# Running products in blocks of 8 joined in runs of four, and the second stage two blocks behind the first

## The chip, the cores and the metric

The kernel runs on one core of one Trainium2 chip. The metric is device time in microseconds of one execution; a stated time is the median of several runs. The engines named below are TensorE (PE; its weight loads are PEld), VectorE (DVE), ScalarE (ACT), GpSimd (POOL) and SyncE (SP), which here issues nearly all DMAs.

## The reference

There are 4 batches x 8 heads, 768 tokens and 48 channels per head. Each head keeps a complex 48x48 state that decays by a complex factor per channel and token:

```
scale = min(mag, 0.999) / (mag + 1e-6)        # mag = |a_re + i a_im|
a     = (a_re, a_im) * scale
for t in range(768):
    S    = a[t] * S  (complex, per channel)  + k[t] v[t]^T   (into the real part)
    y[t] = q[t] . Re(S)
x   = y as (3072 tokens, 384)
out = ((x @ w_a) * (x @ w_b)) @ w_out          # 384 -> 1536 -> 384
```

## The kernel before, in words

**Units.** The work is cut into 12 units u: 2 pairs of batches, each with 6 chunks of 128 tokens. A unit goes through two parts, attention and feed-forward. In attention the recurrence is replaced by matmuls: with P the running product of the factors `a` inside a chunk, the queries are multiplied by P and the keys divided by it, so that scores inside the chunk are q' . k', masked, and the state of the earlier chunks enters as one more matmul.

**`prep(u)`** makes P, on VectorE with help of ScalarE. A unit's factors are 128 partitions x 768 (six groups G of 128 tokens), in real and imaginary planes, plus a negated one (tile `z`). The first multiplication into `z` is L212, the negation L214. Then blocks of SUB = 16 tokens are multiplied up: for i from 1 to 15, one product of 192 elements (L228, into the tile `pr`) and one sum of 96 (L234) carry all 48 blocks of a unit (NB) one token further. In unit 0 each is done in two halves. Then the blocks are joined: 8 times (NSB), one after the other, a product of 24 elements (L255, `pb`) and a sum of 12 (L261, `b_t`) multiply the last value of a block into the carried state, for the six groups at once. L276 and L281 multiply every block's running products by the carried state. L284 to L308 make 1/P with ScalarE's help, L312 multiplies the keys, and L296 multiplies queries and keys by P into the tile `qk`. The last L296 ends the unit's prep.

**`scale(u)`** (L179 to L194) makes the factor `scale` of the next unit and is stepped along inside the loop over i.

**`stack(u)`** (L336) copies `qk` to the tile `stk`, in which each head has its own rows, by 10 DMAs on SP's queue (20 for units 0 and 1). **`attn(u)`** is a list of 12 or 18 pieces: scores (L369, masked by L372), transposes (L380, L384), outputs (L409, L413, with the rest in L418) and state (L426, L433).

**Feed-forward.** A pass over unit w has 12 blocks f of 128 hidden channels. The first stage (`gemm1`, L470) is 18 matmuls of 256 columns into the PSUM tile `ab`; ScalarE and VectorE then multiply the two halves and split the result in a high and a low part: `h_t` (L478, L479), `hh` (L480), `hl` (L481). The second stage (`gemm2`, L488) is 6 matmuls of 384 columns that add block f into the output tiles `o`. LAG = 3 says that the second stage of a block is issued when the first stage of the third block after it has been issued; HB = 4 is the number of buffers of `hh` and of `hl`.

**Weights** come packed and are split into a high and a low part at the start (`split_weights`): three VectorE instructions per piece (L135, L137, L139 into `o_sb`, 36 pieces, three per block f), a copy on ScalarE (L143), two matmuls (L148, L149) and a copy (L150). Pieces of 6 blocks are written ahead of the first attention, the others during pass 0.

**Order.** The program is written as an interleaving: in pass w stand the 12 blocks of unit w, the pieces of attention of unit w + 1, and the prep of unit w + 2 or w + 3, which a generator hands out in portions; the number after each `yield` is the cost that the portion is counted with. From that the tile framework's scheduler makes one order per engine, with priorities (`high_priority`) for what follows a matmul. Ahead of the attention of unit 1 stand WARM = 8 matmuls (L659, two records each) that read unit 1's `qk` and whose result nobody reads.

Of the kernel before, what the change touches and what calls it, by code (L numbers as in the profile page):

```python
# [8 lines left out]
F32 = mybir.dt.float32  # L9
# [5 lines left out]
ALU = mybir.AluOpType  # L15
# [7 lines left out]
NU = NBP * NCH  # L23
NJ = 3
G = 2 * NJ
SUB = 16
NSB = C // SUB
W = G * C
NB = G * NSB
PAIRS = [[2, NB], [2 * NB, SUB // 2], [1, 2]]  # L30
LIFT = 56
LN2 = 0.6931471805599453
# [8 lines left out]
RUN = 2 * TOK + 2  # L41
NF = DF // 128
KS = 2 * D
LAG = 3
EARLY = 2
WARM = 8
HB = 4
O_BUFS = 3
CONV_ON_AB = 7
NCHK = NU * G + NU + 1  # L50
# [9 lines left out]
def view(ap, offset, dims):  # L60
    return bass.AP(tensor=ap.tensor, offset=ap.offset + offset, ap=[list(ap.ap[0])] + dims)


def at_(i):
    return i // 2 * 2 * NB + i % 2


@with_exitstack
def tile_kernel(ctx: ExitStack, tc: tile.TileContext, a_d, qk_d, v_d, w_d, qn_d, kn_d, vn_d, an_d, out_d):
    nc = tc.nc  # L70
    vec, act, pe, sync = nc.vector, nc.scalar, nc.tensor, nc.sync
# [6 lines left out]
    small = fast.enter_context(tc.tile_pool(name="small", bufs=2))  # L78
# [119 lines left out]
    def rescaled(c):  # L198
        return c % 2 == 1 and c + 1 < NCH

    def prep(u):
# [7 lines left out]
        zz = z[:]  # L209

        for k in (1, 0):
            vec.tensor_tensor(out=view(zz, (1 + k) * W, PAIRS), in0=a_t[:, k].rearrange("p (b i e) -> p b i e", e=2, i=SUB // 2),  # L212
                              in1=sc.rearrange("p (b i e) -> p b i e", e=2, i=SUB // 2), op=ALU.mult)
        act.activation(out=z[:, 0], in_=z[:, 2], func=AF.Copy, scale=-1.0)  # L214
        yield 1700
        sg = scale(u + 1, a_tiles[u + 1], a_t) if 0 < u < NU - 1 else iter(())


        zb = z.rearrange("p s (j b e) -> p s j b e", j=SUB // 2, e=2)

        def tok(s, i, o, n):
            return zb[:, s, i // 2, o:o + n, i % 2]

        parts = [(p * NB // 2, NB // 2) for p in range(2)] if u == 0 else [(0, NB)]
        for i in range(1, SUB):
            pr = small.tile([128, 2, 2, NB], F32, name="pr", bufs=1)
            for o, n in parts:
                vec.tensor_tensor(  # L228
                    out=pr[:, :, :, o:o + n],
                    in0=view(zz, W + at_(i) + 2 * o, [[W, 2], [-W, 2], [2, n]]),  # L230
                    in1=tok(slice(1, 3), i - 1, o, n).unsqueeze(1).broadcast_to([128, 2, 2, n]),
                    op=ALU.mult)
            for o, n in parts:
                vec.tensor_tensor(out=tok(slice(1, 3), i, o, n), in0=pr[:, :, 0, o:o + n],  # L234
                                  in1=pr[:, :, 1, o:o + n], op=ALU.add)
            yield 440 + (next(sg, 0) if i > 3 else 0)
        for _ in sg:
            pass
        vec.tensor_scalar(out=tok(0, SUB - 1, 0, NB), in0=tok(2, SUB - 1, 0, NB), scalar1=-1.0,
                          scalar2=None, op0=ALU.mult)  # L240


        if c == 0:
            b_t = small.tile([128, 3, G, NSB], F32, name="b_t")
            vec.memset(b_t[:, 1, :, 0], 1.0)
            vec.memset(b_t[:, 2, :, 0], 0.0)
        else:
            b_t = bnext.pop(u)
# [1 line left out]
        if c + 1 < NCH:  # L250
            bn = bnext[u + 1] = small.tile([128, 3, G, NSB], F32, name="b_t")
        b8 = bn[:, 1:3, :, 0] if bn is not None and not rescaled(c) else small.tile([128, 2, G], F32, name="b8")[:]
        for sb in range(NSB):
            pb = small.tile([128, 2, 2, G], F32, name="pb")
            vec.tensor_tensor(  # L255
                out=pb,
                in0=view(zz, W + at_(SUB - 1) + 2 * sb, [[W, 2], [-W, 2], [2 * NSB, G]]),
                in1=b_t[:, 1:3, :, sb].unsqueeze(1).broadcast_to([128, 2, 2, G]),
                op=ALU.mult)
            dst = b_t[:, 1:3, :, sb + 1] if sb + 1 < NSB else b8  # L260
            vec.tensor_tensor(out=dst, in0=pb[:, :, 0], in1=pb[:, :, 1], op=ALU.add)  # L261
        vec.tensor_scalar(out=b_t[:, 0], in0=b_t[:, 2], scalar1=-1.0, scalar2=None, op0=ALU.mult)
        n2 = small.tile([128, 2, G], F32, name="n2")
        vec.tensor_tensor(out=n2, in0=b8, in1=b8, op=ALU.mult)
# [4 lines left out]
            act.activation(out=rho, in_=rho, func=AF.Exp, scale=-0.5, bias=b_rsq)  # L269
        yield 1600  # L270

        bb = b_t[:]
        for k in range(2):
            pz = a_t
            for s in range(2):
                vec.tensor_tensor(  # L276
                    out=pz[:, s].rearrange("p (j b e) -> p j b e", j=SUB // 2, e=2), in0=zb[:, 1 + s],
                    in1=view(bb, (1 + k - s) * NB, [[0, SUB // 2], [1, NB], [0, 2]]), op=ALU.mult)
            yield 1900

            vec.tensor_tensor(out=z[:, k].rearrange("p (b i e) -> p b i e", e=2, i=SUB // 2),  # L281
                              in0=view(pz[:], 0, PAIRS), in1=view(pz[:], W, PAIRS), op=ALU.add)
            yield 870
        act.activation(out=a_t, in_=z[:, 0:2], func=AF.Square)  # L284
        if rescaled(c):
            vec.tensor_tensor(out=bn[:, 1:3, :, 0], in0=b8,
                              in1=rho[:].unsqueeze(1).broadcast_to([128, 2, G]), op=ALU.mult)
# [13 lines left out]
        if u < EARLY:  # L301
            for k in range(2):
# [6 lines left out]
                                 op0=ALU.subtract, op1=ALU.mult, reverse0=True)  # L309
# [154 lines left out]
    def gemm1(f, xh, xl, ps_ab=ps_ab, moe=moe):  # L464
# [9 lines left out]
        h_t = moe.tile([128, TOK], F32, name="h_t")  # L474
        hh = moe.tile([128, TOK], F32, name="hh", bufs=HB)
        hl = moe.tile([128, TOK], F32, name="hl", bufs=HB)
        with tc.high_priority(offset=MOE_FIRST):
# [129 lines left out]
    ws = split_weights()  # L607
    drain(scale(0, a_tiles[0], z_first))
    drain(prep(0))
    stack(0)  # L610
    load_qk(1)
# [19 lines left out]
    for w in range(NU):  # L631
# [18 lines left out]
        for f in range(NF):  # L650
# [13 lines left out]
            slot()  # L664
            if len(pend) > LAG:
                second()
# [81 lines left out]
```

## Time and profile before

| what | value |
|---|---|
| median of 3 runs | 704.42 us (704.12 to 704.51) |
| the profiled execution | 705.48 us |
| its span, first to last instruction | 703.8 us |
| TensorE busy in the span | 655.8 us, 93%, 5854 matmul records |
| weight loads busy | 608.9 us, 87% |
| VectorE busy | 565.7 us, 80%, 1413 instructions |
| ScalarE busy | 310.4 us, 44%, 618 instructions |
| granted TensorE clock, mean | 0.965 |

A busy share is a mean over the whole span; the kernel has a start, in which weights are split and units 0 and 1 are prepared, a long middle, and an end without prep. So the profile is read by stretches of time: the table of stretches gives the busy time of each engine in each. A line of the trace's order in time gives start, length, engine, line, operation, the tile written and those read, and in brackets the engine's idle time just before with what ended it. "x16" merges 16 neighbours. Matmuls overlap, so that their records are longer than the distance from one to the next.

### The profile page before, as it was taken

To read this page: it belongs to the slowest core of one execution; us is meant where nothing else is said; L and a number is where in the kernel's file an instruction comes from. 1 tells how busy PE (TensorE), PEld (TensorE's weight loads), DVE (VectorE), ACT (ScalarE), POOL (GpSimd) and SP (SyncE) were. 2 spreads that over 40 slices of the span, in tenths; PEclk is the share of its full clock that TensorE was granted. 3 is DMA by queue.
4 is the path that set the end of the run, shared out by engine and by line. 5 is a ranking of instruction groups with operands and counts; after the bars stand their busy time and mean duration, and the time that the engine had idled before them with its cause. 6 is when DMAs were issued, how large, how long until landed. Compare 5 with 4: busy or idle time off the path is not lost.

```text
span 703.8 us, 14498 instructions
## 1 busy us (share of the span) xinstructions
PE 655.8 (93%) x5854; PEld 608.9 (87%) x5854; DVE 565.7 (80%) x1413; ACT 310.4 (44%) x618; POOL 5.6 (1%) x11
## 2 busy tenths in 40 slices
PE   3657999699999999999999999999999999999996
PEld 1224889599899899999899999999999999999996
DVE  6998899898888898889889989899899997233221
ACT  6347665534625525436346355362463323231221
POOL 3000000000000000000000000000000000000000
PEclk9566999899999999999999999999999999999999
DMA  8963300421512413305216043051250320400000
GB/s 320 401 253 88 118 1 1 137 75 45 159 31 75 129 32 108 110 17 158 65 26 190 16 125 95 31 163 42 76 157 2 102 87 9 114 23 2 23 1 28
DMA packets 32090, 63.95 MB, mean 91 GB/s; under 512 B 3984, under 2 KB 10640, under 8 KB 32016
## 3 DMA queue, kind: packets, MB, share of 16 engines
q1 hardware_dynamic: 28560, 58.23, 26.6%
q10 hardware_dynamic: 3456, 4.72, 1.9%
q8 instruction: 48, 0.79, 0.5%
q14 instruction: 26, 0.21, 0.1%
HBM read 39.32 MB, written 4.72 MB: 63 GB/s over the span
## 4 chain that ended last, share of the span: by engine, by line
PE 46%; DVE 42%; ACT 5%; DMA 3%; issue 3%; SPq 1%; DVEq 0%; ACTq 0%
PE ab L470 19%; PE o L488 9%; PE xp L409 6%; DVE pr L228 5%; PE pm L369 5%; DVE a_t L276 4%; DVE qk L296 4%; PE pm L426 3%; DVE h_t L479 3%; DVE z L234 3%; DVE hl L481 3%; DMA stk<-qk 2%; DVE z L281 2%; PE pm L380 2%; DVE pb L255 2%
## 5 line engine op out<-in xcount | busy, mean ns | idle before, releaser
L470 PE MATMUL ab<-xh,w 128*128 128x256 f32 x1728 | 334.1, 283 | 0.0
L470 PEld LDWEIGHTS ab<-xh,w 128*128 128x128 f32 x1728 | 275.6, 189 | 1.9 <-issue 1.2
L470 PE MATMUL ab<-xl,w 128*128 128x256 f32 x864 | 243.0, 281 | 0.0
L470 PEld LDWEIGHTS ab<-xl,w 128*128 128x128 f32 x864 | 162.5, 188 | 0.7 <-issue 0.4
L488 PE MATMUL o<-w,hh 128*128 128x384 f32 x576 | 152.5, 344 | 0.0
L478 ACT COPY h_t<-ab 128x256 f32<-128x256 f32 x144 | 53.4, 371 | 175.4 <-PE ab L470 175.1
L479 DVE TENSOR_TENSOR h_t<-ab,h_t 128x256 f32<-128x256 f32 x144 | 60.5, 420 | 58.3 <-ACT h_t L478 57.7
L488 PEld LDWEIGHTS o<-w,hh 128*128 128x128 f32 x576 | 96.3, 188 | 3.2 <-issue 3.2
L488 PE MATMUL o<-w,hl 128*128 128x384 f32 x288 | 97.7, 339 | 0.0
L480 ACT CAST hh<-h_t 128x256 fp32r<-128x256 f32 x144 | 58.1, 404 | 78.4 <-DVE h_t L479 77.9
L481 DVE TENSOR_TENSOR hl<-h_t,hh 128x256 fp32r<-128x256 f32 x144 | 60.6, 421 | 16.8 <-ACT hh L480 16.5
L228 DVE TENSOR_TENSOR pr<-z 128x192 f32<-128x192 f32 (+1 forms) x195 | 65.2, 341 | 5.6 <-ACT z L214 1.3
L369 PE MATMUL pm<-stk 128*128 128x128 f32 x384 | 56.4, 284 | 3.4 <-DMA stk<-qk 3.4
L369 PEld LDWEIGHTS pm<-stk 128*128 128x128 f32 x384 | 50.2, 195 | 8.1 <-issue 7.6
L148 PE MATMUL ab<-o_sb,ident 128*128 128x384 f32 x42 | 30.1, 817 | 27.9 <-DVE o_sb L139 27.9
L488 PEld LDWEIGHTS o<-w,hl 128*128 128x128 f32 x288 | 54.1, 188 | 0.2
L234 DVE TENSOR_TENSOR z<-pr 128x96 f32<-128x96 f32 (+1 forms) x195 | 47.2, 249 | 3.7
L276 DVE TENSOR_TENSOR a_t<-z,b_t 128x768 f32<-128x768 f32 x48 | 45.5, 953 | 0.0
L409 PE MATMUL xp<-am,v_t 128*32 128x128 f32 x768 | 43.1, 277 | 0.5 <-DVE am L372 0.5
L148 PEld LDWEIGHTS ab<-o_sb,ident 128*128 128x128 f32 x42 | 10.6, 292 | 37.6 <-DVE o_sb L139 27.9
L296 DVE TENSOR_TENSOR qk<-qk,z 128x1536 f32<-128x1536 f32 (+1 forms) x28 | 42.6, 1523 | 0.1
L372 DVE TENSOR_TENSOR am<-pm,mask 128x512 f32<-128x512 f32 x48 | 32.9, 686 | 6.0 <-PE pm L369 5.7
(100 smaller groups left out, 753.9 us busy)
## 6 DMA issues: line engine op xcount, KB each, us to landing
w<-in_dram SPq DMA_DIRECT2D x36, 384.0 KB, 8.0
qk<-in_dram SPq DMA_DIRECT2D x12, 768.0 KB, 4.9
a_t<-in_dram SPq DMA_DIRECT2D x11, 768.0 KB, 4.4
stk<-qk SPq DMA_DIRECT2D x42, 192.0 KB, 3.3
v_t<-in_dram SPq DMA_DIRECT2D x24, 256.0 KB, 2.7
out_dram<-o_sb ACTq DMA_DIRECT2D x24, 192.0 KB, 2.0
stk<-qk SPq DMA_DIRECT2D x18, 192.8 KB, 3.3
stk<-qk SPq DMA_DIRECT2D x14, 128.0 KB, 3.0
```

Of the source, the lines that this page charges most:

```text
L228: vec.tensor_tensor(out=pr[:, :, :, o:o + n], in0=view(zz, W + at_(i) + 2 * o, [[W, 2], [-W, 2], [2, n]]), in1=tok(slice(1, 3), i - 1, o, ...
L234: vec.tensor_tensor(out=tok(slice(1, 3), i, o, n), in0=pr[:, :, 0, o:o + n], in1=pr[:, :, 1, o:o + n], op=ALU.add)
L276: vec.tensor_tensor(out=pz[:, s].rearrange("p (j b e) -> p j b e", j=SUB // 2, e=2), in0=zb[:, 1 + s], in1=view(bb, (1 + k - s) * NB, [[0, ...
L296: vec.tensor_tensor(out=qk4[:, :, k, x0:x1], in0=qk4[:, :, 1, x0:x1], in1=z[:, k].rearrange("p (j t) -> p j t", j=NJ).unsqueeze(2).broadca ...
L369: pe.matmul(out=sp[:, h4], lhsT=stk[:, h, ks], rhs=stk[:, h, qs], start=True, stop=True)
L409: pe.matmul(out=xp[qd * 32:(qd + 1) * 32, ti], lhsT=l, rhs=rr, start=st, stop=sp_, tile_position=(0, qd * 32), skip_group_check=True)
L470: pe.matmul(out=ab[:, m * TOK:(m + 1) * TOK], lhsT=r(w_ab(f, part, m * NJ + i)), rhs=r(xt[:, i, :]), start=n == 0, stop=n == 8)
L478: act.copy(out=h_t, in_=ab[:, 0:TOK])
L479: vec.tensor_tensor(out=h_t, in0=ab[:, TOK:2 * TOK], in1=h_t, op=ALU.mult)
L480: act.copy(out=r(hh), in_=h_t)
L481: vec.tensor_tensor(out=r(hl), in0=h_t, in1=hh, op=ALU.subtract)
L488: pe.matmul(out=os_[tt][:, 0:DM], lhsT=r(ht[:, ts]), rhs=r(w_t[f, 2][:, part, :]), start=(f == 0 and n == 0), stop=(f == NF - 1 and n == 2))
```

## The change

Three things change.

**Blocks of 8.** SUB goes from 16 to 8. The loop over i has 7 steps in place of 15, each over 96 blocks (NB) in place of 48: products of 384 elements and sums of 192. The number of blocks in a group of 128 tokens (NSB) goes from 8 to 16.

**The join in runs of four.** The 16 blocks of a group are four runs of RUNS = 4. First the running products inside every run are made for all 24 runs (NG) at once, in the new tile `c_t`: a copy, three times a product of 96 and a sum of 48, and a negation. Then the state is carried from run to run, four times a product of 24 and a sum of 12. At last the state inside the runs is filled in: two products and one sum of 144 elements. `joined` is the new helper that writes a product and a sum.

**The second stage.** LAG goes from 3 to 2 and HB from 4 to 3: the second stage of a block is issued after the first stage of the second block behind it, and `hh` and `hl` have three buffers each.

The count after a step's `yield` goes from 440 to 880, and `scale` is stepped along from the second step on.

```diff
-SUB = 16
+SUB = 8
+RUNS = 4
 NSB = C // SUB
 W = G * C
 NB = G * NSB
+NG = NB // RUNS
...
-LAG = 3
+LAG = 2
...
-HB = 4
+HB = 3
...
-            yield 440 + (next(sg, 0) if i > 3 else 0)
+            yield 880 + (next(sg, 0) if i > 1 else 0)
...
-        for sb in range(NSB):
-            pb = small.tile([128, 2, 2, G], F32, name="pb")
-            vec.tensor_tensor(
-                out=pb,
-                in0=view(zz, W + at_(SUB - 1) + 2 * sb, [[W, 2], [-W, 2], [2 * NSB, G]]),
-                in1=b_t[:, 1:3, :, sb].unsqueeze(1).broadcast_to([128, 2, 2, G]),
-                op=ALU.mult)
-            dst = b_t[:, 1:3, :, sb + 1] if sb + 1 < NSB else b8
-            vec.tensor_tensor(out=dst, in0=pb[:, :, 0], in1=pb[:, :, 1], op=ALU.add)
+        c_t = small.tile([128, 3, RUNS, NG], F32, name="c_t", bufs=1)
+        cc, bb = c_t[:], b_t[:]
+
+        def joined(out, x, y, n):
+            pb = small.tile([128, 2, 2, NG], F32, name="pb")
+            vec.tensor_tensor(out=pb[:, :, :, 0:n], in0=x,
+                              in1=y.unsqueeze(1).broadcast_to([128, 2, 2, n]), op=ALU.mult)
+            vec.tensor_tensor(out=out, in0=pb[:, :, 0, 0:n], in1=pb[:, :, 1, 0:n], op=ALU.add)
+
+        vec.tensor_copy(out=c_t[:, 1:3, 0], in_=view(zz, W + at_(SUB - 1), [[W, 2], [2 * RUNS, NG]]))
+        for k in range(1, RUNS):
+            joined(c_t[:, 1:3, k], view(zz, W + at_(SUB - 1) + 2 * k, [[W, 2], [-W, 2], [2 * RUNS, NG]]),
+                   c_t[:, 1:3, k - 1], NG)
+        vec.tensor_scalar(out=c_t[:, 0], in0=c_t[:, 2], scalar1=-1.0, scalar2=None, op0=ALU.mult)
+        n_run = NSB // RUNS
+        for k in range(n_run):
+            dst = b_t[:, 1:3, :, (k + 1) * RUNS] if k + 1 < n_run else b8
+            joined(dst, view(cc, NB + (RUNS - 1) * NG + k, [[NB, 2], [-NB, 2], [n_run, G]]), b_t[:, 1:3, :, k * RUNS], G)
+        pr = small.tile([128, 2, 2, RUNS - 1, NG], F32, name="pr", bufs=1)
+        for k in range(2):
+            vec.tensor_tensor(out=pr[:, k], in0=view(cc, (1 + k) * NB, [[-NB, 2], [NG, RUNS - 1], [1, NG]]),
+                              in1=view(bb, NB, [[NB, 2], [0, RUNS - 1], [RUNS, NG]]), op=ALU.mult)
+        vec.tensor_tensor(out=view(bb, NB + 1, [[NB, 2], [1, RUNS - 1], [RUNS, NG]]),
+                          in0=pr[:, :, 0], in1=pr[:, :, 1], op=ALU.add)
```

The scheduler makes a new order for every engine from the changed program. Lines behind the join lie 16 further down in the changed kernel: L296 becomes L312, L470 becomes L486, L488 becomes L504, L659 becomes L675; L228 and L234 become L230 and L236, and the weight splitting's L135, L137, L139 become L137, L139, L141. What the new order does on VectorE and TensorE around the end of unit 1's prep is shown in rows in the prediction, each row an instruction with its line, its operation, the tile it writes and those it reads.

More of the change, by code (lines that the diff above doesn't have):

```diff
@@ L270, in prep @@
         yield 1600
-        bb = b_t[:]
         for k in range(2):
```

## The prediction

> **What bounds the kernel now.** I read the page for the span, then the table of stretches, the order in time of TensorE and VectorE around the places where TensorE stops, and the matmuls of one feed-forward pass (12 blocks of 18 matmuls) per stretch. The table's columns: length, then busy time and instructions of PE, PEld, DVE, ACT and POOL, then TensorE's clock, DMA share and GB/s.
>
> ```profile
> span 703.8 us, 14498 instructions
> ...
> 0.00:61.00 61.00, 32.12 (x57) 14.54 (x57) 54.02 (x173) 32.07 (x62) 5.60 (x11) 0.72 0.79 293
> ...
> 80.00:126.00 46.00, 45.26 (x298) 40.60 (x297) 43.42 (x126) 28.76 (x60) 0.00 (x0) 1.00 0.08 25
> ...
> 154.00:330.00 176.00, 172.83 (x1633) 166.68 (x1632) 155.16 (x369) 80.42 (x155) 0.00 (x0) 1.00 0.28 83
> ```
>
> Up to 61 us VectorE is the full engine and TensorE waits. After 154 us TensorE is full. In between stands one long stop, in TensorE's order in time (start, length, what, idle time before it):
>
> ```profile
> 125.02 0.34 PE L488 MATMUL o<-w,hl 128*128 128x384 f32 x1
> 130.78 6.41 PE L659 MATMUL pm<-qk,ident 128*128 128x256 f32 x16 [5.42 <-DVE qk L296]
> ```
>
> TensorE has run out of blocks and waits 5.42 us for VectorE's last product of unit 1. So up to 130.7 us each microsecond off VectorE's queue counts; what TensorE still has to do behind the stop counts too. Then the passes, cut at their first matmul (216 matmul records, first length, then their busy time):
>
> ```profile
> 154.20:205.30 51.10, 28.57 (x216) 26.93 (x216) 1.00 0.28 81
> 205.30:257.65 52.35, 29.13 (x216) 27.11 (x216) 1.00 0.27 79
> 257.65:310.20 52.55, 28.68 (x216) 27.07 (x217) 1.00 0.28 83
> 310.20:358.05 47.85, 27.74 (x216) 26.84 (x217) 1.00 0.30 86
> ...
> 508.60:559.00 50.40, 27.80 (x216) 26.52 (x217) 1.00 0.27 75
> ...
> 610.10:656.05 45.95, 27.45 (x216) 26.76 (x217) 1.00 0.03 10
> ```
>
> A pass with 18 attention pieces beside it takes 50.40 where nothing is late; passes 1, 2 and 3 take 0.70, 1.95 and 2.15 more. Pass 4 has 12 pieces and takes 1.90 more than the other pass with 12, at 610 us. These 6.7 us are all that faster VectorE work can bring after 154 us, and the reason stands ahead of the scores:
>
> ```profile
> 180.75 0.46 PE L369 MATMUL pm<-stk 128*128 128x128 f32 x2 [1.25 <-DMA stk<-qk]
> ...
> 230.37 0.46 PE L369 MATMUL pm<-stk 128*128 128x128 f32 x2 [0.86 <-DMA stk<-qk]
> ...
> 280.42 0.46 PE L369 MATMUL pm<-stk 128*128 128x128 f32 x2 [1.05 <-DMA stk<-qk]
> ```
>
> The copy qk to stk starts when VectorE ends a unit's last product; there VectorE is late. From pass 5 on there is no such wait.
>
> **Running products.** VectorE's order in time, first unit 0 (two halves, weight work between), then unit 1 among other work, then unit 2 with nothing between:
>
> ```profile
> 19.87 0.43 DVE L228 TENSOR_TENSOR pr<-z 128x96 f32<-128x96 f32 x2 [0.30 <-ACT z L214]
> 20.22 0.33 DVE L234 TENSOR_TENSOR z<-pr 128x48 f32<-128x48 f32 x2
> 20.46 0.55 DVE L139 SCALAR_TENSOR_TENSOR o_sb<-w,o_sb 128x384 uint32<-128x384 uint32 x1
> ```
> ```profile
> 85.84 0.35 DVE L228 TENSOR_TENSOR pr<-z 128x192 f32<-128x192 f32 x1
> 86.11 0.35 DVE L135 TENSOR_SCALAR o_sb<-w 128x384 uint32<-128x384 uint32 x1
> 86.38 0.25 DVE L234 TENSOR_TENSOR z<-pr 128x96 f32<-128x96 f32 x1
> 86.54 0.55 DVE L137 SCALAR_TENSOR_TENSOR o_sb<-w,o_sb 128x384 uint32<-128x384 uint32 x1
> 87.01 0.35 DVE L228 TENSOR_TENSOR pr<-z 128x192 f32<-128x192 f32 x1
> ```
> ```profile
> 132.69 0.36 DVE L228 TENSOR_TENSOR pr<-z 128x192 f32<-128x192 f32 x1
> 133.09 0.26 DVE L234 TENSOR_TENSOR z<-pr 128x96 f32<-128x96 f32 x1
> 133.38 0.36 DVE L228 TENSOR_TENSOR pr<-z 128x192 f32<-128x192 f32 x1
> ```
>
> What an instruction costs is the step from its start to the next start: among other work 0.27 for 192 elements (85.84 to 86.11), 0.16 for 96, 0.47 for 384 (86.54 to 87.01), less than the durations; where the next one reads its result, 0.40 and 0.29.
>
> Unit 0: 15 steps of 0.35 + 0.24 = 0.59 make 8.9. After, 7 steps of twice 192 and twice 96 elements, 2 x (0.27 + 0.16) = 0.86, make 6.0: -2.9. Unit 1: 15 x (0.27 + 0.16) = 6.5 against 7 x (0.47 + 0.27) = 5.2: -1.3.
>
> The Trainium skill (VectorE: DVE Perf Modes, The DRAIN you can't avoid) says that the next op does not start until the pipe is empty, so that each instruction would cost its whole duration. Here 86.11 stands against it: the next instruction starts 0.27 after one that lasts 0.35. By the rule the saving would be larger; that is a rival below.
>
> **The join.** Before, 8 products of 24 elements and 8 sums of 12 per unit:
>
> ```profile
> 34.99 0.20 DVE L255 TENSOR_TENSOR pb<-z,b_t 128x24 f32<-128x24 f32 x1
> 35.10 0.55 DVE L139 SCALAR_TENSOR_TENSOR o_sb<-w,o_sb 128x384 uint32<-128x384 uint32 x1
> ...
> 35.57 0.17 DVE L261 TENSOR_TENSOR b_t<-pb 128x12 f32<-128x12 f32 x1
> 35.65 0.55 DVE L137 SCALAR_TENSOR_TENSOR o_sb<-w,o_sb 128x384 uint32<-128x384 uint32 x1
> ```
> ```profile
> 151.36 0.20 DVE L255 TENSOR_TENSOR pb<-z,b_t 128x24 f32<-128x24 f32 x1
> 151.59 0.18 DVE L261 TENSOR_TENSOR b_t<-pb 128x12 f32<-128x12 f32 x1
> ```
>
> Among other work a pair costs 0.11 + 0.08, 8 make 1.5. After: a copy and a negation (0.1 each), 3 products of 96 (0.16) and 3 sums of 48 (0.12, between 0.08 and 0.16), 4 of the old pairs (0.8), 3 instructions of 144 elements (0.22, between 0.16 and 0.27): 2.5, so +1.0 per unit, an estimate from these rows. Units 0 and 1 together save 2.9 + 1.3 - 2.0 = 2.2. That is the low bound of what the stop at 130.78 gains.
>
> **What the new order moves on VectorE.** Around unit 1's last product (qk<-qk,z), before:
>
> ```order
> L479 TENSOR_TENSOR h_t<-ab,h_t 128x256
> L290 TENSOR_TENSOR a_t<-a_t 128x768
> L481 TENSOR_TENSOR hl<-h_t,hh 128x256
> L306 TENSOR_TENSOR a_t<-a_t 128x768
> L308 SCALAR_TENSOR_TENSOR a_t<-a_t 128x768
> L312 TENSOR_TENSOR qk<-qk,a_t 128x3x256
> L296 TENSOR_TENSOR qk<-qk,z 128x3x256 x2
> L212 TENSOR_TENSOR z<-a_t,sc 128x48x8x2 x2
> ```
>
> and after, where o_sb<-w is weight splitting and L312 is the old L296:
>
> ```order
> L312 TENSOR_TENSOR qk<-qk,z 128x3x256
> L137 TENSOR_SCALAR o_sb<-w_194 128x384
> L312 TENSOR_TENSOR qk<-qk,z 128x3x256
> L495 TENSOR_TENSOR h_t<-ab,h_t 128x256
> L139 SCALAR_TENSOR_TENSOR o_sb<-w_194,o_sb 128x384
> L137 TENSOR_SCALAR o_sb<-w_196 128x384
> L497 TENSOR_TENSOR hl<-h_t,hh 128x256
> L141 SCALAR_TENSOR_TENSOR o_sb<-w_194,o_sb 128x384
> L139 SCALAR_TENSOR_TENSOR o_sb<-w_196,o_sb 128x384
> L137 TENSOR_SCALAR o_sb<-w_198 128x384
> L141 SCALAR_TENSOR_TENSOR o_sb<-w_196,o_sb 128x384
> L139 SCALAR_TENSOR_TENSOR o_sb<-w_198,o_sb 128x384
> ```
>
> Before, all weight splitting and 11 pairs h_t, hl stood ahead of that product; now 8 weight instructions (one more follows these rows) and one pair stand behind it. The 8 cost 2 x 0.27 + 6 x 0.47 = 3.4, the pair (256 elements, between 0.27 and 0.47) 0.7. Other weight instructions now stand between L290 and L306, where before VectorE waited:
>
> ```profile
> 125.79 0.96 DVE L306 TENSOR_TENSOR a_t<-a_t 128x768 f32<-128x768 f32 x1 [1.70 <-ACT a_t L292]
> ```
>
> I take 1.0 of these 1.70 as filled, bounds 0 and 1.70. The stop so ends 2.2 + 3.4 + 0.7 + 1.0 = 7.3 earlier, bounds 2.2 and 8.0. What went behind is not late again: TensorE first runs 6.41 us of L659, longer than these 4.1.
>
> **What the second stage's new place moves on TensorE.** Around the same stop, o<-w the second stage and pm<-qk the matmuls that wait. Before:
>
> ```order
> L488 MATMUL o_794<-w_960,hh 128x384 x2
> L488 MATMUL o_794<-w_960,hl 128x384
> L488 MATMUL o_795<-w_960,hh 128x384 x2
> L488 MATMUL o_795<-w_960,hl 128x384
> L488 MATMUL o_794<-w_1019,hh 128x384 x2
> L488 MATMUL o_794<-w_1019,hl 128x384
> L488 MATMUL o_795<-w_1019,hh 128x384 x2
> L488 MATMUL o_795<-w_1019,hl 128x384
> ```
>
> These are blocks 8 and 9, block 10 follows, then the stop. After:
>
> ```order
> L504 MATMUL o_741<-w_905,hh 128x384 x2
> L504 MATMUL o_741<-w_905,hl 128x384
> L504 MATMUL o_742<-w_905,hh 128x384 x2
> L504 MATMUL o_742<-w_905,hl 128x384
> L675 MATMUL pm<-qk,ident 128x256 x8
> L150 MATMUL pm<-o_sb,ident 128x384
> L151 MATMUL pm<-w_1100,nident 128x384
> ```
>
> Only block 8 is done ahead of the stop; blocks 9 and 10 come behind it, where TensorE is full. The chain of waits gives what a block costs there, first and second stage:
>
> ```profile
> 613.50 2.12 PE ab L470 x18
> 615.62 1.05 PE o L488 x6
> ```
>
> So 2 x 1.05 = 2.1 is given back, and the start gains 7.3 - 2.1 = 5.2.
>
> **Later units.** With nothing between, 15 x (0.40 + 0.29) = 10.4 becomes 7 steps of about 0.59 (a 384-element instruction, 0.55, plus the same 0.04) + 0.40, that is 6.9: -3.4. The join, 16 x 0.23 = 3.7, becomes about 4.8: +1.1. So a unit saves 2.3 there, and 1.3 - 1.0 = 0.3 among other work; I take 1.1, nearer the second, since VectorE is busy 155.16 of 176. VectorE enters unit 2 only 7.3 - 3.4 = 3.9 earlier, plus 1.1 makes 5.0, and TensorE 5.2: the wait of pass 1 stays. In passes 2, 3 and 4 the copies come 1.1 earlier each time, which they can use up (1.95, 2.15, 1.90): -3.3, bounds 0 and 6.7. Passes from 5 on gain nothing: TensorE hides VectorE's work. Fewer buffers for hh and hl cost nothing: block f writes where f-3 was read, and that second stage now stands ahead of block f's first.
>
> Sum: 703.8 - 5.2 - 3.3 = 695.3 of span. The profiled execution took 705.48, 1.7 outside its span; the median is 704.42, so I predict 704.42 - 8.5 = 695.9.
>
> **Rivals.** (1) The order's gain is lost (TensorE waits for the weight work put behind): the stop gains 2.2 and gives back 2.1, leaving 704.4 - 0.1 - 3.3 = 701.0. For it: block 11's weights now stand between the stop and the first scores. Against: the 6.41 us of cover.
>
> (2) Nothing: VectorE's time is hidden and the score waits are set by the copies: 704.4. Against: 5.42 us named after VectorE.
>
> (3) Slower: the second stage two blocks behind finds hl late, and TensorE waits in each block. From a first stage's end it now has 1.05 + 2.12 + 1.05 + 2.12 = 6.3 us. The slowest block in the late passes:
>
> ```profile
> 372.76 0.28 PE L470 MATMUL ab<-xh,w 128*128 128x256 f32 x1
> ```
> ```profile
> 377.99 0.42 DVE L481 TENSOR_TENSOR hl<-h_t,hh 128x256 fp32r<-128x256 f32 x1
> ```
>
> 373.04 to 378.41 is 5.4, so 0.9 is left. It decides from 6.3 on: at a mean of 6.5 the 96 blocks of passes 0 to 7 lose 0.2 each, 19 us, and the time is 715.1.
>
> (4) Whole durations count, with no overlap between starts:
>
> ```profile
> L228 DVE TENSOR_TENSOR pr<-z 128x192 f32<-128x192 f32 x165 | 58.9, 357 | 5.3 <-ACT z L214 1.0
> ...
> L234 DVE TENSOR_TENSOR z<-pr 128x96 f32<-128x96 f32 x165 | 42.3, 257 | 3.7
> ...
> L187 DVE TENSOR_TENSOR z<-z 128x384 f32<-128x384 f32 x2 | 1.1, 551 | 0.0
> ```
>
> A unit's steps go from 15 x 0.614 = 9.2 to 7 x 0.908 = 6.4, the join +1.1: -1.7 per unit; unit 0 from 15 x (0.43 + 0.33) = 11.4 to 7 x 2 x 0.614 = 8.6, with the join -1.7 too. The stop gains 3.4 + 5.1 - 2.1 = 6.4, the passes 3 x 1.7 = 5.1: 692.9. Against: the starts in every row above. The skill's rule on DRAIN would give this.
>
> **How the numbers follow.** Forecast 0.62, rival 1 0.17, rival 4 0.05: faster 0.84. Rival 2: same 0.07. Rival 3: slower 0.09. About 0.2% (1.4 us) is what a measurement of this kernel can tell from no change. The range: full fill and all 6.7 give 704.4 - 5.9 - 6.7 = 691.8, rival 1 gives 701.0; 691.5 to 701.5.
>
> **What would show it.** Right: L659 starts near 123.5; two second stages follow it; the pass from about 149 us is unchanged, the next three nearer 50.4, 50.4 and 46; steps of 0.47 and 0.27 in the products. Wrong: a gap ahead of the second stage named after hl, weight matmuls waiting behind L659, or score waits as long as before in passes 2 to 4.

## The result and the profile after

The changed kernel takes 698.99 us (median of 6 runs, 698.31 to 699.92) against 704.81 for the kernel before beside it: a ratio of 0.9913, 95% interval 0.99 to 0.9925. That is faster by about 6 us, inside the range, 3.1 us above the forecast of 695.9. The profiled execution took 698.89 us.

The page of the changed kernel, its span and its busy times:

```profile
span 697.2 us, 14316 instructions
...
PE 655.2 (94%) x5854; PEld 610.8 (88%) x5854; DVE 551.8 (79%) x1241; ACT 308.9 (44%) x618; POOL 5.6 (1%) x11
...
PE 64%; DVE 27%; ACT 4%; DMA 2%; issue 1%; SPq 1%; ACTq 0%; DVEq 0%
```

The last of these lines is the chain of work that ended last: 64% of it is now TensorE. The same three stretches as before the change, and the one in which the long stop had been:

```profile
0.00:61.00 61.00, 30.07 (x53) 13.20 (x53) 53.54 (x145) 32.67 (x62) 5.59 (x11) 0.74 0.81 297
80.00:126.00 46.00, 45.98 (x293) 40.85 (x292) 44.76 (x113) 26.53 (x58) 0.00 (x0) 1.00 0.16 47
154.00:330.00 176.00, 173.25 (x1670) 166.45 (x1669) 157.53 (x330) 82.65 (x157) 0.00 (x0) 1.00 0.30 89
```
```profile
130.00:140.00 10.00, 10.00 (x152) 9.08 (x150) 9.78 (x21) 7.22 (x12) 0.00 (x0) 1.00 0.29 85
```

The kernel before had this in the last of them (fourth column from the end: the granted clock):

```profile
130.00:140.00 10.00, 9.22 (x29) 7.08 (x30) 9.05 (x23) 6.07 (x9) 0.00 (x0) 0.69 0.53 161
```

So behind the stop TensorE also ran at a clock of 0.69, and that went with the stop. The same holds for the other kernels below: in the kernel before and three more, with a stop of 4.5 to 5.4 us in this place, the 16 records behind it took 5.7 to 6.4 us; in the kernels without one they took 3.6 to 3.7. TensorE's order in time around the place of the stop (L675 is the old L659), and the longest wait that is left:

```profile
122.59 0.34 PE L504 MATMUL o<-w,hl 128*128 128x384 f32 x1
122.76 3.68 PE L675 MATMUL pm<-qk,ident 128*128 128x256 f32 x16
...
175.66 0.46 PE L385 MATMUL pm<-stk 128*128 128x128 f32 x2 [1.66 <-DMA stk<-qk]
```

There is no idle time ahead of 122.76: the stop of 5.42 is gone. The 16 records take 3.68 where they took 6.41. The passes, cut at their first matmul (1 to 4, then 8 and 10 as passes with 18 and 12 pieces in which little is late):

```profile
144.85:199.45 54.60, 29.80 (x216) 1.00 0.25 76
199.45:252.70 53.25, 29.84 (x216) 1.00 0.27 78
252.70:303.70 51.00, 28.68 (x216) 1.00 0.29 86
303.70:350.75 47.05, 27.93 (x216) 1.00 0.30 88
502.35:553.25 50.90, 28.14 (x216) 1.00 0.23 66
603.80:650.20 46.40, 27.94 (x216) 1.00 0.03 10
```

Pass 1 is longer than before, 2 longer, 3 and 4 shorter. The late passes, which should not have changed, are longer: 46.40 against 45.95. In pass 11, where nothing runs beside the blocks, the first matmuls of two blocks in a row stand here, before and after:

```profile
656.11 0.28 PE L470 MATMUL ab<-xh,w 128*128 128x256 f32 x1
...
659.28 0.28 PE L470 MATMUL ab<-xh,w 128*128 128x256 f32 x1
```
```profile
650.22 0.28 PE L486 MATMUL ab<-xh,w 128*128 128x256 f32 x1
...
653.41 0.28 PE L486 MATMUL ab<-xh,w 128*128 128x256 f32 x1
```

A block went from 3.167 to 3.193 us (medians of the steps in that pass). All of it is in the first stage: from one of its matmuls to the next it is now 119.2 ns instead of 117.6, and the second stage is as before. 144 blocks at 0.026 make up to 3.7 us that no step of the prediction had. The accounts of the two profiled executions, in spans, at equal work (with LAG 2, six second-stage matmuls fewer are done when pass 1 starts, and six more from there on; a block's six count 1.05):

```
                              forecast   measured
up to the start of pass 1       -5.2       -8.3    (154.25 -> 144.88, less 1.05)
pass 1                           0         +1.4    (51.12 -> 54.58, less 2 x 1.05)
passes 2, 3, 4                  -3.3       -1.4    (152.72 -> 151.33)
passes 5 to 11                   0         +1.7
span                            -8.5       -6.6    (703.8 -> 697.2)
```

### The profile page after: what moved, and what is told of

It is laid out like the page before. It is cut to its first block, busy times and chain, and to the rows that moved or that the text cites. A ratio compares the mean times of both kernels' runs of the same rounds, so it can differ in the third digit from the quotient of the medians.

```text
span 697.2 us, 14316 instructions
## 1 busy us (share of the span) xinstructions
PE 655.2 (94%) x5854; PEld 610.8 (88%) x5854; DVE 551.8 (79%) x1241; ACT 308.9 (44%) x618; POOL 5.6 (1%) x11
## 4 chain that ended last, share of the span: by engine, by line
PE 64%; DVE 27%; ACT 4%; DMA 2%; issue 1%; SPq 1%; ACTq 0%; DVEq 0%
PE ab L486 30%; PE o L504 14%; PE xp L425 6%; PE pm L385 5%; PE pm L442 4%; DVE a_t L292 3%; DVE pr L230 2%; DVE qk L312 2%; DVE h_t L495 2%; PE pm L396 2%; DVE hl L497 2%; PE pm L150 2%; DVE z L297 2%; DVE pb L260 1%; DVE z L236 1%
## 5 line engine op out<-in xcount | busy, mean ns | idle before, releaser
L486 PE MATMUL ab<-xh,w 128*128 128x256 f32 x1728 | 339.0, 285 | 0.0
L486 PEld LDWEIGHTS ab<-xh,w 128*128 128x128 f32 x1728 | 278.1, 190 | 1.8 <-issue 1.4
L486 PE MATMUL ab<-xl,w 128*128 128x256 f32 x864 | 245.1, 284 | 0.0
L486 PEld LDWEIGHTS ab<-xl,w 128*128 128x128 f32 x864 | 164.4, 190 | 0.5 <-issue 0.2
L504 PE MATMUL o<-w,hh 128*128 128x384 f32 x576 | 152.3, 344 | 0.0
L504 PEld LDWEIGHTS o<-w,hh 128*128 128x128 f32 x576 | 96.8, 190 | 3.7 <-issue 3.0
L504 PE MATMUL o<-w,hl 128*128 128x384 f32 x288 | 96.9, 336 | 0.0
L385 PE MATMUL pm<-stk 128*128 128x128 f32 x384 | 54.4, 279 | 2.7 <-DMA stk<-qk 2.7
L504 PEld LDWEIGHTS o<-w,hl 128*128 128x128 f32 x288 | 54.1, 188 | 0.0
L385 PEld LDWEIGHTS pm<-stk 128*128 128x128 f32 x384 | 48.7, 191 | 5.9 <-issue 4.8
L230 DVE TENSOR_TENSOR pr<-z 128x384 f32<-128x384 f32 (+1 forms) x91 | 47.1, 524 | 2.4 <-ACT z L216 0.8
L425 PE MATMUL xp<-am,v_t 128*32 128x128 f32 x768 | 42.5, 277 | 1.3 <-DVE am L388 1.2
L312 DVE TENSOR_TENSOR qk<-qk,z 128x1536 f32<-128x1536 f32 (+1 forms) x28 | 42.7, 1524 | 0.1
L425 PE MATMUL xp<-stk,u 128*32 128x128 f32 x640 | 34.4, 273 | 0.0
```

The source lines that it names most:

```text
L230: vec.tensor_tensor(out=pr[:, :, :, o:o + n], in0=view(zz, W + at_(i) + 2 * o, [[W, 2], [-W, 2], [2, n]]), in1=tok(slice(1, 3), i - 1, o, ...
L312: vec.tensor_tensor(out=qk4[:, :, k, x0:x1], in0=qk4[:, :, 1, x0:x1], in1=z[:, k].rearrange("p (j t) -> p j t", j=NJ).unsqueeze(2).broadca ...
L385: pe.matmul(out=sp[:, h4], lhsT=stk[:, h, ks], rhs=stk[:, h, qs], start=True, stop=True)
L425: pe.matmul(out=xp[qd * 32:(qd + 1) * 32, ti], lhsT=l, rhs=rr, start=st, stop=sp_, tile_position=(0, qd * 32), skip_group_check=True)
L486: pe.matmul(out=ab[:, m * TOK:(m + 1) * TOK], lhsT=r(w_ab(f, part, m * NJ + i)), rhs=r(xt[:, i, :]), start=n == 0, stop=n == 8)
L504: pe.matmul(out=os_[tt][:, 0:DM], lhsT=r(ht[:, ts]), rhs=r(w_t[f, 2][:, part, :]), start=(f == 0 and n == 0), stop=(f == NF - 1 and n == 2))
```

## The experiments

Two questions were open: what slowed the first stage, and what carries the gain of the start through to the end. All times beside a ratio are medians; the ratio is against the kernel before on the same chip.

**What slowed the first stage.** Theory W: LAG 2 makes TensorE look at more semaphores. Theory S: the new tiles of the join and the larger `pr` moved all tiles behind them, `xh` and `xl` among them.

```
kernel before:  LAG = 3 -> 2    HB = 4 -> 3
```

> The kernel before with only LAG 3 to 2 and HB 4 to 3; running products and join as before. Theory W (the second stage closer behind the first makes TensorE look at two more semaphores per block, and that slows the first stage): in a clean block of the last pass the step between first-stage matmuls rises from 117.6 to about 120 ns, the block from 3.167 to about 3.193 us, the time by up to 144 x 0.026 = 3.7 us, to about 707.5. Theory S (the changed place of tiles, from the new join's tiles and SUB 8, slows it): step and block unchanged, time within 1 us of before. Rival 3 of the prediction (hl late): gaps named after hl, time above 710.

It took 703.35 (ratio 0.9969, 0.9958 to 0.9981). The clean block stayed at 3.167. W is wrong, and so was the expectation that without it LAG and HB change less than 1 us: alone they are worth 2.2 us. VectorE ends unit 3's last product 1.9 earlier in this kernel (226.82 before, 224.92 here); why the scheduler's order comes out better was not taken apart.

```
changed kernel:  HB = 3 -> 4, h_t with bufs=1,
-  c_t = small.tile([128, 3, RUNS, NG], F32, name="c_t", bufs=1)
+  c_t = a_t[:, 0, 0:3 * NB].rearrange("p (s r n) -> p s r n", s=3, r=RUNS)
second kernel: the same, and LAG = 2 -> 3
```

> The changed kernel with HB back at 4 and LAG still 2; to make room the join's c_t lies in a_t and h_t has one buffer. Theory W: clean block stays at 3.193 us, time about that of the changed kernel, 699. Theory B (three buffers for hh and hl put the writes of one block where another is read): block back at 3.167 us and about 695.5.

> The changed kernel with LAG 3 and HB 4 as before, c_t in a_t, h_t with one buffer: running products and join alone. Theory W: clean block back at 3.167 us, passes from 5 on at the length they had before, time about 699 - 3.5 = 695.5. Theory S: block stays at 3.193 us and the time at about 699.

HB 4 took 698.70 (0.9905, 0.9888 to 0.9923), LAG 3 took 699.75 (0.9918, 0.9902 to 0.9935). In both the clean block is 3.207, a third value, so W and B both fall. The tiles moved once more: without the 1152 bytes of `c_t` ahead of it, `xh` starts 64 bytes past a multiple of 256, and the step between first-stage matmuls is 118.9 ns, which leaves S standing. That step alone would make the block shorter than 3.193; what makes it longer lies in the second stage and at the change between the stages, and was not taken apart. The running products and the join alone are worth about 6 us, with this slower block; LAG 2 brings about 1 more, which the two intervals do not separate.

```
   changed kernel (and, in a second one, the kernel before), ahead of x_cur = new_x():
+  pad = moe.tile([128, 16], F32, name="pad", bufs=1)
+  nc.gpsimd.memset(pad, 0.0)
```

> The changed kernel with 64 bytes put ahead of xh, xl, h_t, hh and hl in each partition: xh then starts at byte 208640, a multiple of 128 as in the kernel before (204928), where in the changed kernel it starts at 208576, which is 64 past one. Theory S (where xh and xl start sets the step of the first stage): a clean block of the last pass goes back from 3.193 to 3.167 us, and 144 blocks x 0.026 = 3.7 us come off: about 695.3. Rival (the step is set by something else that the change brought): 3.193 us and about 699.

> The kernel before with the same 64 bytes ahead of xh: xh starts at 204992, 64 past a multiple of 128. Theory S: the step of the first stage rises from 117.6 to about 120 ns, a clean block from 3.167 to about 3.19 us, the time by up to 3.7 us, less where TensorE waits anyway in passes 0 to 4: about 707. Rival: block unchanged, time unchanged.

First matmuls of blocks in pass 11, of the changed kernel with 64 bytes and of the kernel before with 64 bytes:

```profile
648.55 0.28 PE L486 MATMUL ab<-xh,w 128*128 128x256 f32 x1
...
658.07 0.28 PE L486 MATMUL ab<-xh,w 128*128 128x256 f32 x1
```
```profile
657.99 0.28 PE L470 MATMUL ab<-xh,w 128*128 128x256 f32 x1
...
661.18 0.28 PE L470 MATMUL ab<-xh,w 128*128 128x256 f32 x1
```

The first pair is three blocks apart, 9.52 / 3 = 3.17 each; the second is one, 3.19. So 64 bytes turn the longer step on and off, and S is shown. The kernel before loses by them what was expected: 708.82 (1.0053, 1.0038 to 1.0067), that is 3.7 us. The changed kernel gains less: 697.68 (0.99, 0.9886 to 0.9914), about 1 us less than without them, 1.6 by the spans (697.2 and 695.6). Of these, passes 5 to 11 give 0.9; elsewhere TensorE waits longer instead. This is the fastest kernel of the study.

```
   changed kernel, behind the last second stage (probe_pairs: xh and xl in the order of a first stage)
+  for o in (0, 1, 4, 8, 16, 24, 32, 48, 64, 80, 96, 112, 0):
+      for n in range(18):
+          pe.matmul(out=ps[:, 0:TOK], lhsT=r(w_ab(NF - 1, n % 2, n // 3)), rhs=r(xf[:, o:o + TOK]), ...)
+  for n, st, so in ((96, 1, 1), (96, 2, 1), (96, 3, 1), (96, 4, 1), ...):
+      vec.tensor_tensor(out=view(u0, 0, [[so, n]]), in0=view(sf, 0, [[st, n]]), in1=view(uf, 0, [[1, n]]), op=ALU.mult)
```

> The changed kernel with work added behind its last second stage: 13 groups of 18 matmuls of 256 columns with weights as in a first stage, the columns read from xh at offsets of 0, 4, 16, 32, 64, 96, 128, 192, 256, 320, 384, 448 and 0 bytes, then on VectorE products of 24 to 384 elements with one operand read or the result written at strides of 1 to 16 elements. Theory S: the step of a matmul depends on the offset, about 120 ns at 0 and 117.6 where the start is a multiple of 128 bytes (64, 192, 320, 448), by about 2%; rival: one step for all. For VectorE: by the theory that strides make the join dear, 96 elements at stride 8 take about 0.33 us against 0.25 at stride 1 or 2; rival (it is the number of dimensions or the broadcast operand): no difference between strides.

> The changed kernel with 16 groups of 18 matmuls added behind its last second stage, in the order of a first stage (high part with xh, high part with xl, low part with xh), xh and xl each read from starts of 192, 0, 64 and 128 bytes past a multiple of 256. If each matmul's own start sets its step, the groups' means are mixes of 119.5, 117.8, 118.7 and 114.8 ns (two parts xh, one part xl). If the first stage of the kernel before (both at 128, 117.6) differs from the earlier groups (128, 114.7) because two tensors alternate, both at 128 gives 117.6.

Two groups of 18 matmuls of the first probe, read from starts of 0 and 192 bytes past that of `xh`:

```profile
690.27:692.41 2.14, 2.14 (x18) 1.00 0.34 118
...
705.24:707.31 2.07, 2.07 (x20) 1.00 0.00 0
```

The same 18 matmuls take 2.14 or 2.07 us. The steps, worked out from the starts (mean from the third step of a group on), by the start of the columns past a multiple of 256 bytes:

```
start          192          0         64        128      208   224   32    196
ns a step   119.5 119.3  117.8 117.8 118.7 118.7 114.8 114.7  116.8 116.8 119.9 122.3
both tensors (second probe)
            119.5        117.8     118.7     113.3
```

Starts 256 bytes apart give the same step, to 0.2 ns. Two expectations of the second probe fell. Where `xh` and `xl` start differently, the step is not the mix of their own: with `xh` at 128 and `xl` at 64 it is 119.2, where the mix gives 116.0. And the kernel before has `xh` and `xl` at 128 and a step of 117.6, the probes 113.3 to 114.8 there; two tensors in turn do not explain it, and it stays open.

**What carries the gain to the end.** Theory V: VectorE's last product of units 2 and 3 and the copies behind it. Rival T: TensorE, which is full from 80 us on.

```
changed kernel:  WARM = 8 -> 0
```

> The changed kernel without the 16 matmul records that stand behind unit 1's last product (WARM 0; their results are used by nothing). If TensorE has no stop left there, as the trace of the changed kernel says, their 3.68 us lie on the path whole: about 695.3. If the stop was only filled by them, VectorE's data being late all the same, TensorE waits instead and the time stays near 699; if they keep the clock up, the granted clock between 120 and 154 us falls from 1.00 towards 0.9 and the time rises.

It took 699.20 (0.9903, 0.9886 to 0.9921): nothing, though TensorE came to pass 1 1.7 us earlier and had ten second-stage matmuls more behind it by then. VectorE's start of unit 3's last product, in the changed kernel and in this one:

```profile
217.77 1.75 DVE L312 TENSOR_TENSOR qk<-qk,z 128x1536 f32<-128x1536 f32 x1
```
```profile
217.78 1.75 DVE L312 TENSOR_TENSOR qk<-qk,z 128x1536 f32<-128x1536 f32 x1
```

VectorE did not notice. TensorE was still 2.9 us ahead at the start of pass 3 and lost 2.3 of it in that pass, which took 53.3 instead of 51.0. Its scores meet unit 4's copy late, where the changed kernel has no wait. Below stand this wait and the busy time of the 128 output matmuls (L425) of pass 3, without the 16 records and then with them; from start to start they take 5.0 and 3.9 us:

```profile
271.61 0.46 PE L385 MATMUL pm<-stk 128*128 128x128 f32 x2 [0.27 <-DMA stk<-qk]
...
249.80:303.10 53.30, 5.53 (x128) 1.00 0.27 82
```
```profile
252.70:303.70 51.00, 4.12 (x128) 1.00 0.29 86
```

The wait is the smaller part. Where the copies come late, TensorE's order takes the scores two at a time between parts of blocks and breaks up the outputs too. In passes 1 to 3 and 6 to 9 of all kernels, the outputs take 4.6 to 5.4 us from start to start wherever a score waits for a copy, and such a pass takes 52.4 us or more at equal work; where the pieces stand in whole groups, the outputs take 3.9. Why the same matmuls take longer in the broken order was not taken apart. So T falls for this part, and V needs two more things: unit 4's copy, and the broken order beside the wait.

```
changed kernel, the old join over 16 blocks:
-  (runs of four, carried state, products into b_t)
+  for sb in range(NSB):
+      pb = (product of 24 with b_t[..., sb]);  b_t[..., sb + 1] = (sum of 12)
second kernel:  RUNS = 4 -> 2, pb with bufs=1
```

> The changed kernel with blocks of 8 and LAG 2, but the join as before the change: 16 products of 24 elements and 16 sums of 12 one after the other, no runs of four (xh kept at 64 past a multiple of 128). By the prediction's own terms the plain join costs 16 x 0.19 = 3.0 us of VectorE among other work against 2.5 of runs of four (3.4 with the durations measured since), and 16 x 0.46 = 7.4 against 4.8 with nothing between: unit 2 gets 2.6 us later, which pass 1 or 2 shows, the start hardly changes: about 700 to 702. If VectorE's time in the join is hidden throughout, the time stays at 699.

> The changed kernel with runs of two in place of four (and one buffer for pb): 1 + 8 dependent pairs of product and sum in the join instead of 3 + 4, the same blocks of 8, xh at the same place. The plain join with 16 pairs took 716.7 against 699. Theory D (what counts up to pass 3 is the number of dependent VectorE instructions, since one weight instruction slips in behind each of them): 17.7 us for 9 more pairs, 2.0 for a pair, so 2 more pairs make 3.9 and the time is about 703, with about 4 more weight instructions ahead of unit 0's last join instruction. Rival (what counts is VectorE's own work): 4 more instructions of 0.2 us and less for smaller ones, under 0.5 per unit: 699 to 700.5.

The old join took 716.74 (1.0169, 1.0156 to 1.0182), 17.7 us more than with runs of four and 12 more than before: blocks of 8 without the runs would have been a loss. VectorE in unit 0's join, with the old join and with runs of four:

```profile
30.33 0.19 DVE L258 TENSOR_TENSOR pb<-z,b_t 128x24 f32<-128x24 f32 x1
30.44 0.55 DVE L139 SCALAR_TENSOR_TENSOR o_sb<-w,o_sb 128x384 uint32<-128x384 uint32 x1
30.91 0.17 DVE L264 TENSOR_TENSOR b_t<-pb 128x12 f32<-128x12 f32 x1
30.99 0.55 DVE L141 SCALAR_TENSOR_TENSOR o_sb<-w,o_sb 128x384 uint32<-128x384 uint32 x1
```
```profile
29.93 0.32 DVE L260 TENSOR_TENSOR pb<-z,c_t 128x96 f32<-128x96 f32 x1
30.17 0.54 DVE L139 SCALAR_TENSOR_TENSOR o_sb<-w,o_sb 128x384 uint32<-128x384 uint32 x1
30.63 0.20 DVE L262 TENSOR_TENSOR c_t<-pb 128x48 f32<-128x48 f32 x1
30.75 0.55 DVE L141 SCALAR_TENSOR_TENSOR o_sb<-w,o_sb 128x384 uint32<-128x384 uint32 x1
```

Behind nearly every join instruction, which the next one must wait for, the order has one weight instruction. In unit 0's join (from the negation ahead of it to the one behind it) stand 31 of them with the old join, 16 with runs of four, 15 before the change, and the join lasts 16.5, 9.5 and 7.6 us. The stop ahead of L663 is back in the old-join kernel's waits:

```profile
PE pm L663 <- DVE qk L298: 4.5, 1, 4.5
```

Runs of two took 698.89 (0.9912, 0.9894 to 0.993), where theory D had 703. Its local half held: 20 weight instructions in unit 0's join, as many more as foreseen, and unit 1's last product 1.3 later. Its price for the whole did not: unit 3 is 1.2 later and the end not at all.

```
changed kernel, the join as a scan by doubling over the 16 blocks, all in a_t:
+  d = 1
+  while d < NSB:   # c[i] = c[i] * c[i - d]
+      (product of 2 x 2 x 6 x (16 - d), sum of half, its negation);  d *= 2
+  (products with the carried state into b_t and b8)
```

> The changed kernel with the join as a scan by doubling over the 16 blocks (distances 1, 2, 4, 8), then the carried state multiplied in: 4 dependent pairs of up to 360 and 180 elements and one pair for the state, about 12 dependent instructions in place of about 18, whose elements are three times as many. xh starts at a multiple of 256. Compare with the changed kernel with 64 bytes put in, 697.7. Theory D: some 6 dependent instructions fewer at 1.0 each, up to -6: 692 to 695. Rival (own work): 4 x (0.53 + 0.35) + 0.9 = 4.4 us of durations against about 4.0 now, no gain or a small loss: 697.5 to 699.

It took 703.44 (0.9981, 0.9969 to 0.9992), 5.8 more than the changed kernel with `xh` at a like place. Its join holds 12 weight instructions in unit 0 instead of 16, but its own instructions last 6.45 us a unit against 4.76, more than expected, and unit 3 ends 6 us later. So neither the dependent instructions nor VectorE's own work alone orders these kernels. What runs along with the time is the end of unit 3's last product (in the table, in us; light is the last test, below). In the kernel before, this is its row:

```profile
225.07 1.75 DVE L296 TENSOR_TENSOR qk<-qk,z 128x1536 f32<-128x1536 f32 x1
```

```
kernel                 unit 1's last  unit 3's last   time     xh past a multiple of 256
changed, light            122.1          205.3        700.1      192
changed, HB 4             121.4          218.2        698.7       64
changed, 64 bytes         122.4          219.3        697.7        0
changed                   122.7          219.5        699.0      192
changed, no WARM          122.6          219.5        699.2      192
changed, LAG 3            122.5          219.7        699.8       64
changed, runs of two      123.9          220.7        698.9      192
before, LAG 2             130.0          224.9        703.4      128
changed, scan             127.0          225.6        703.4        0
before, 64 bytes          129.6          226.0        708.8      192
before                    130.7          226.8        704.8      128
changed, old join         136.7          234.0        716.7      192
```

From 234 down to about 220 the time falls with it, but for the start of `xh`. Unit 1's end orders the kernels nearly as well, so the table does not show that unit 3 alone decides. Whether more VectorE time could bring more was the last test:

```
changed kernel:
-  for i in range(1, SUB):
+  for i in range(1, SUB if u < 2 else 4):
```

> The changed kernel with 4 of the 7 product steps left out in units 2 to 11 (tokens 4 to 7 of each block are not multiplied up; units 0 and 1 are whole), so about 4 x 0.9 = 3.6 us less on VectorE per unit, join and order untouched. In the changed kernel passes 1 to 4 take 54.6, 53.3, 51.0 and 47.1 against 50.6 and 46.4 of the late passes of the same kind, 8 us more, and the kernel without the 16 matmul records, which gave TensorE 3.7 us earlier, did not end earlier. Theory V (VectorE's last product of units 2 and 3, and the copy behind it, set passes 1 to 4): most of these 8 us go, about 692 to 694. Rival T (they are TensorE's own, from the attention pieces and their small waits, whatever VectorE does): 698 to 699. Passes from 5 on: unchanged by either.

It took 700.06 (0.993, 0.9916 to 0.9943). V is right as far as it goes: passes 1 and 2 take 52.8 and 51.4 instead of 54.6 and 53.3, and pass 4 starts at 299.4 instead of 303.7. So below 220 the time no longer follows unit 3, which ends 14 us earlier here. What the early passes gain is lost again, in passes that both theories had as unchanged. Three passes of this kernel, the wait in the longest, and VectorE there:

```profile
396.30:448.60 52.30, 28.11 (x217) 1.00 0.26 77
448.60:503.50 54.90, 29.85 (x216) 0.97 0.26 77
503.50:555.70 52.20, 28.13 (x216) 1.00 0.23 64
```
```profile
475.09 0.55 PE L396 MATMUL pm<-ident,stk 96*128 96x96 f32 x4 [2.14 <-DVE am L388]
```
```profile
473.14 0.96 DVE L192 SCALAR_TENSOR_TENSOR a_t<-a_t 128x768 f32<-128x768 f32 x1 [0.47 <-ACT a_t L190]
474.02 0.42 DVE L495 TENSOR_TENSOR h_t<-ab,h_t 128x256 f32<-128x256 f32 x1
474.35 0.68 DVE L388 TENSOR_TENSOR am<-pm,mask 128x512 f32<-128x512 f32 x1
```

The mask `am`, which has to read the PSUM tile `pm` before TensorE may write it again, stands in VectorE's order behind work on a later unit's `scale`, which itself waits for ScalarE. In the longest pass the granted clock fell too, to a mean of 0.97. Each change of the program gives another order; with this one the waits for masks are 0.8 to 2.4 us in each of passes 5 to 8, against at most 0.4 in the changed kernel.

## Why the prediction was right or wrong

That the time came near the forecast is in part luck: by the account above the start gained 3.1 us more than forecast, and everything behind it came out 5.0 worse.

**The bound.** Right. VectorE's last product of unit 1 ended the stop, and the stop went. With the old join, which makes VectorE's chain longer, the stop is back; without the 16 records an earlier TensorE alone brings nothing.

**Product terms.** Right. VectorE's order in time in the changed kernel, a product step of unit 1 among weight work, and an instruction of unit 2's join:

```profile
84.73 0.35 DVE L236 TENSOR_TENSOR z<-pr 128x192 f32<-128x192 f32 x1
85.00 0.35 DVE L137 TENSOR_SCALAR o_sb<-w 128x384 uint32<-128x384 uint32 x1
85.27 0.55 DVE L230 TENSOR_TENSOR pr<-z 128x384 f32<-128x384 f32 x1
85.74 0.55 DVE L139 SCALAR_TENSOR_TENSOR o_sb<-w,o_sb 128x384 uint32<-128x384 uint32 x1
...
152.03 0.42 DVE L275 TENSOR_TENSOR pr<-c_t,b_t 128x144 f32<-128x144 f32 x1
152.37 0.17 DVE L262 TENSOR_TENSOR b_t<-pb 128x12 f32<-128x12 f32 x1
```

The "steps of 0.47 and 0.27" are there: 85.27 to 85.74, 84.73 to 85.00. Summed over the product steps, unit 0 went from 8.7 to 6.1 us (forecast 8.9 to 6.0), unit 1 from 7.1 to 5.5 (6.5 to 5.2).

**The join's +1.0 per unit.** Too small. The prediction priced elements alone, 0.16 for 96 and 0.22 for 144. The groups of the changed kernel (busy, mean ns of one):

```profile
L260 DVE TENSOR_TENSOR pb<-z,c_t 128x96 f32<-128x96 f32 x36 | 12.0, 333 | 0.9
L275 DVE TENSOR_TENSOR pr<-c_t,b_t 128x144 f32<-128x144 f32 x24 | 9.9, 415 | 0.0
```

They last 333 and 415 ns, where the row of 96 elements in the prediction has 257, because operands are read with a stride: the probe has 324 for 96 elements at stride 8, and by its 1.8 ns an element 144 make 410 (last section). The steps are 0.24 (29.93 to 30.17, above) and 0.34 (152.03 to 152.37): 3 x 0.08 + 3 x 0.12 makes 0.6 more per unit. Summed over unit 0's join instructions, the steps are 1.6 before and 3.0 now: +1.4. Products and join of units 0 and 1 together so gave 1.4, not 2.2.

**The order's part of the start (8 weight instructions, one pair, 1.0 of a wait).** Right in kind: of 108 weight instructions 100 stand ahead of that product now, and one pair less. L675 starts at 122.76, 8.0 before 130.78, where the prediction had 7.3. That this is so near is in part two errors that cancel: products and join gave 0.8 less, and VectorE's idle time up to that product fell from 13.2 to 10.4 us, 2.8 where the prediction took 1.0.

**TensorE behind the stop.** The 2.1 given back are there (54 second-stage matmuls ahead of L675 where 66 stood ahead of L659). Missed: the prediction took the 6.41 us of L659 as a fixed length. Its clock was low behind the stop, and without the stop it is 3.68. So the start is 8.3 instead of 5.2; but the kernel without these matmuls ended no earlier, so what they gave is not what reached the end.

**The copies in passes 2, 3 and 4: -3.3.** This is the step that failed, together with "passes from 5 on gain nothing". VectorE did what the term asked for and more: unit 3's last product came 7.3 earlier than before, unit 1's 8.1. For pass 1 the prediction had set 5.0 for unit 2's copies against 5.2 for TensorE; it was 5.1 against 8.3, so pass 1 pays 1.4. At the start of pass 2 TensorE is still 7.0 ahead at equal work, and unit 3's copies, 7.3 earlier, are as late for it as before: the score wait is 1.00 us against 0.86, one of the prediction's own signs of being wrong, and the pass gains nothing (53.3 against 52.4). Only from pass 3 on is the wait gone; passes 3 and 4 gain 1.5 and 0.8. Passes 2 to 4 together gain 1.4 instead of 3.3. What the term left out is that a larger lead of TensorE makes the same copies late again; the next late copy takes it back, as in the kernel without the 16 records.

**Passes from 5 on: 0.** Measured +1.7. The start of `xh` makes 0.9 of it by the two changed kernels with and without 64 bytes, and 1.8 by the two kernels before, so it is half or more of it. The waits for masks moved as well (0.9 us in passes 6 to 8, where 0.2 stood before; none in passes 5 and 9, where it was 1.5); the rest was not taken apart.

**The rivals.** No wait on `hl` stands in the trace of the changed kernel; the second stage of a block starts 1.6 us or more after its `hl`, but for the very last block (0.5), so the third rival did not happen, and LAG 2 was even a small gain. The first (order's gain lost) and the second (nothing) are refuted by the start. The fourth, whole durations, would have had a larger gain; the steps in the fences above stay shorter than the durations. The section of the Trainium skill that the prediction names for it (VectorE: DVE Perf Modes, The DRAIN you can't avoid) also says that a next op that is not held starts earlier, which the prediction left out; the steps of 0.27 behind 0.35 agree with that.

## What to carry to other kernels

Where one engine feeds another unit by unit, follow the time of the hand-overs, not busy sums: here the time ran along with the end of unit 3's last product, down to about 220 us. A chain of dependent small instructions costs, besides itself, whatever a scheduler puts between them, so count its links; time freed in one stage can come back in a later one, as a wait or as an order that breaks work into smaller pieces. And after any change of tiles compare a clean stretch of the main loop before and after: a matmul that was not touched can have another step.

## What the runs showed of the hardware

**A matmul's step depends on where its columns start.** 256 columns of 4 bytes took 114.7 to 122.3 ns from one matmul to the next by the start in the partition, and starts 256 bytes apart gave the same step. With two tensors in turn it took 113.3 to 119.5, and not as a mix of the two. In the kernel 64 bytes are worth 0.026 us a block, 3.7 us in the kernel before. The Trainium skill (SBUF — State Buffer, Operand start alignment) treats an operand's start as a matter of legality and says of its own runs that they timed nothing; here it has a price.

**VectorE slows at strides of 3 and more.** Products of 96 elements with one operand at stride 1, 2, 3, 4, 8 and 16 took 258, 258, 280, 324, 324 and 314 ns; with the result written at stride 4, 327; 192 elements took 359 at stride 1 and 2 and 495 at 4 and 8. Between 96 and 192 elements that is 1.05 ns an element against 1.8. The Trainium skill (SBUF — State Buffer, Door 1: The DMA port swizzle) says that SBUF has lines of 16 bytes and that full bandwidth needs at least two hits in a line. Worked out from that, at 4 bytes stride 2 is free and stride 4 is not, and these numbers agree; read as a free stride, the "4 fp32" of the same note does not.
